# A dense layer's last chunk of 96 units made with 128 columns of weights, and value groups moved to steps 2, 4 and 5

## The chip, the cores and the metric

The kernel runs on one core of a Trainium2 chip. The metric is the device time of one execution in microseconds (us). An execution that is profiled gives a trace: each engine's instructions with their start and duration. The engines are PE (TensorE, matrix products; PEld is its loading of weights), DVE (VectorE), ACT (ScalarE), POOL (GpSimd) and SP (SyncE, which here only issues DMAs).

## What is computed

An input of 2048 tokens with 512 features goes through two layers of recurrent-memory attention, each followed by a dense layer. Cut to what matters:

```
def attention(x, mem):                      # 32 heads of 128; M = 8 memory rows
    for s in range(64):                     # segments of 32 tokens
        h = concat(mem, x[32*s : 32*s+32])  # 40 rows
        q, k, v = h @ Wq, h @ Wk, h @ Wv    # 512 -> 4096 each
        o = (softmax(mask(q @ k.T) * 128**-0.5) @ v) @ Wo
        mem = o[:8]                         # goes on to the next segment
        out[32*s : 32*s+32] = o[8:]
def dense(x):                               # w1: 512 x 1376, w2: 1376 x 512
    return relu(x @ w1) @ w2
x = x + attention(norm(x), mem0);  x = x + dense(norm(x))
x = x + attention(norm(x), mem0);  x = x + dense(norm(x))
```

Both layers use the same weights. A segment needs the memory that the segment before it left, so the segments of one layer are made one after the other.

## The kernel before, in words

**Steps.** The program is unrolled into steps 0 to 67. At step k layer 0 makes segment k (to k = 63) and layer 1 makes segment k - 4 (from k = 4), so steps 4 to 63 carry both layers; steps 0 to 3 and 64 to 67 carry one ("single"). Step 0 is `first_step`, the others are calls of `step(k)` (L895). The order of instructions on PE, DVE, SP and POOL is the one in which the code issues them; the order on ACT is left to a scheduler. Each engine works its list in order, so an instruction that waits holds up all that stand behind it on its engine.

**The recurrent chain.** In each step the 32 heads are made in two halves of 16: queries and keys (`qk`, L575; cast to SBUF by ACT, L581, and DVE, L583), scores (`scores`, L609; added onto a mask that DVE copies into PSUM beforehand, L601), softmax (maximum, subtraction and sum on DVE, exponential on ACT L631, multiplication on POOL or DVE L646), the turning of P (first half by a DMA, second half by PE, L656, with copies L660), then the weighted sum of the values (L682), copied to SBUF (L700), and the output projection of the memory rows (`output_mem`, L617). `new_memory` (L812) copies it (wm, L814), turns it by PE (mt, L820), and copies it into HT and HTm, the inputs of the next step's queries and of the memory's values (`memory_values`, L765).

**Fill.** While the softmax of a half runs, PE does work that does not hang on this chain:
- `output_x(k - 1)`: the output projection of the tokens of the step before (L365, L388 or L393). In steps with k % 4 = 1 there is none, because those tokens went along with the memory rows.
- `dense_h(k - 2)` (L507) and `dense_y(k - 2)` (L528): the two products of the dense layer. The 1376 units are cut into 11 chunks, ten of 128 and the last of 96. `dense_h` makes each chunk with four matmuls (one for each 128 of the 512 features), in pieces of chunks 8 to 10 and 0 to 7; each piece lies in one PSUM bank and is taken to SBUF by ACT with a relu, the chunk of 96 by a relu of its own (L515).
- `values0(p, n)` (L306): the values of layer 0's tokens for a pair of segments p (64 tokens) and 1024 of the 4096 columns: a **value group**, eight matmuls of 64 x 512, copied by ACT (L312) and stored by SP in DRAM (vd0[p]), from where `load_values` reads them when the segment's turn comes. Only odd p are needed. Four groups (n = 0, 2, 4, 6) make one p.

**Which step makes which groups** is written out in `values_at` (L800): step 1 has three, step 5 two, then each step with k % 4 = 1 has three (steps 9 to 37) or four (41 to 61). Steps with two or three groups are `split` ("light"): the dense layer's first piece, half of a group, the second scores, the second piece and the remaining groups follow one another. In steps with four, all of `dense_h` comes before the second scores and the groups after them.

**The inputs.** A tile of 128 tokens, xbs[n], is loaded (SP), its moments are made (`moments_x`, DVE, with a pow on POOL), it is normalized (DVE) and turned into xT0[n], by PE for the first tiles and by a DMA for the others. Before, tile n + 3 of step 4n is loaded at step 4n, its moments are made in step 4n + 1 behind the softmax of the second half, it is normalized at the end of step 4n + 2 and turned in step 4n + 3; tile 3 is turned early, in step 1, into another buffer, and once more in step 3.

Of the kernel before, what the change touches and what calls it, by code (L numbers as in the profile page):

```python
# [22 lines left out]
def kernel(  # L23
# [132 lines left out]
    def load_dense():  # L156
        nc.sync.dma_start(out=w1_sb[:], in_=B_w1.rearrange("(c p) f -> p c f", p=128))
        nc.sync.dma_start(out=w2_sb[:, 0:NFC - 1, :],
                          in_=B_w2[0:(NFC - 1) * 128, :].rearrange("(c p) d -> p c d", p=128))
        nc.sync.dma_start(out=w2_sb[0:F_LAST, NFC - 1, :], in_=B_w2[(NFC - 1) * 128:Dff, :])  # L160

    mhalf_t = const.tile([128, 1], F32)
    nc.vector.memset(mhalf_t[:], -0.5)
# [51 lines left out]
    xT0, xnT_tiles, hT_tiles, vd0, vd1, vmds, wm_tiles, wo_tiles, xp_tiles, vp_tiles, obs = {}, {}, {}, {}, {}, {}, {}, {}, {}, {}, {}  # L215

    def stat_tail(stats, of=""):
        mv = wk.tile([128, 2], F32, tag="ln_mv" + of, bufs=2 - len(of), name="mv")
        nc.vector.bn_aggr(out=mv[:], in_=stats[:])
        rstd = wk.tile([128, 1], F32, tag="ln_rstd" + of, bufs=2 - len(of), name="rstd")  # L220
        nc.vector.tensor_scalar_add(out=rstd[:], in0=mv[:, 1:2], scalar1=LN_EPS)
        nc.gpsimd.tensor_tensor(out=rstd[:], in0=rstd[:], in1=mhalf_t[:], op=ALU.pow)
        return mv, rstd

    def normalize(eng, dst, src, mom, lo, hi):
# [12 lines left out]
            nc.tensor.transpose(tp[:, c4, :], xn[:, c4 * 128:(c4 + 1) * 128], ident[:])  # L238
        return tp

    def inputs_T(n, early=False):
        tag, bufs = ("ob", 1) if early else ("xT0", 3)
        xT0[n] = wk.tile([128, NC4, 128], BF, tag=tag, bufs=bufs, name="xT0")
        if n < 3 or early:
            tp = transpose_pe(xbs[n])
            nc.scalar.copy(out=xT0[n][:], in_=tp[:])
        else:
            nc.sync.dma_start_transpose(out=xT0[n][:], in_=xbs[n][:])
# [47 lines left out]
    def values0(p, n, lo=0, hi=NC4, pool=None, stage=None):  # L296
        r = 64 * (p % 2)
        if (n, lo) == (0, 0):
            vd0[p] = dram.tile([4, 2, 64, 512], BF, tag="vd0", bufs=3, name="vd0")
        if lo == 0:  # L300
            pool, tag = (pool, "wo") if pool else (ps_fill, "fill")
            vp_tiles[p, n] = pool.tile([128, 512], F32, tag=tag, name="vp")
        vp = vp_tiles[p, n]
        for c4 in range(lo, hi):
            for j in range(2):
                nc.tensor.matmul(vp[64 * j:64 * j + 64, :], lhsT=xT0[p // 2][:, c4, r:r + 64],  # L306
                                 rhs=Wv_sb[:, c4, (n + j) * 512:(n + j + 1) * 512],
                                 start=(c4 == 0), stop=(c4 == NC4 - 1), tile_position=(0, 64 * j))
        if hi < NC4:
            return  # L310
        vst = wk.tile([128, 512], BF, tag="vst", bufs=5, name="vst")[:] if stage is None else stage
        nc.scalar.copy(out=vst, in_=vp[:])  # L312
        nc.sync.dma_start(out=vd0[p][n // 2].rearrange("j t e -> (j t) e"), in_=vst)
# [95 lines left out]
    def last_rows(k, eng):  # L409


        r = 64 * (LAST - k)
        R = residual(LAST - 1)
        if not last_t:
            last_t["stats"] = wk.tile([128, 2, 6], F32, tag="ln_last", bufs=1, name="stats")
            last_t["mv"] = wk.tile([128, 2], F32, tag="ln_mvl", bufs=1, name="mv")
            last_t["rstd"] = wk.tile([128, 1], F32, tag="ln_rstdl", bufs=1, name="rstd")
        stats, mv, rstd = (last_t[x][r:r + 64] for x in ("stats", "mv", "rstd"))
        nc.vector.bn_stats(out=stats[:, 0, :], in_=R[r:r + 64, 0:256])
        for j in range(2):  # L420
            nc.vector.tensor_copy(out=last_t["stats"][r + 32 * j:r + 32 * j + 32, 1, :],
                                  in_=last_t["stats"][r + 32 - 32 * j:r + 64 - 32 * j, 0, :])
        nc.vector.bn_aggr(out=mv, in_=stats.rearrange("p n s -> p (n s)"))
        nc.vector.tensor_scalar_add(out=rstd, in0=mv[:, 1:2], scalar1=LN_EPS)
        nc.gpsimd.tensor_tensor(out=rstd, in0=rstd, in1=mhalf_t[r:r + 64, :], op=ALU.pow)
        eng.tensor_scalar(out=XN[r:r + 64, 0:256], in0=R[r:r + 64, 0:256], scalar1=mv[:, 0:1], scalar2=rstd[:, 0:1],
                          op0=ALU.subtract, op1=ALU.mult)
# [58 lines left out]

    def dense_h(d, parts=slice(None)):
        if not 0 <= d <= LAST:  # L490
            return
        lo, hi = span(d)
        n = hi - lo

        def cols(c4):
            return xnT_tiles[d + 2][:, c4, lo:hi]

        if not parts.start:
            hT_tiles[d] = wk.tile([128, NFC, 64], BF, tag="hT", bufs=1, name="hT")
        hT = hT_tiles[d]  # L500
        pieces = ((8, NFC), (0, 4), (4, 8)) if d == LAST - 1 else ((8, NFC), (0, 8))
        for f0, f1 in pieces[parts]:
            hp = ps_fill.tile([128, 8, 64], F32, tag="fill", name="hp")
            for fc in range(f0, f1):
                fs = 128 if fc < NFC - 1 else F_LAST
                for c4 in range(NC4):
                    nc.tensor.matmul(hp[0:fs, fc - f0, 0:n], lhsT=w1_sb[:, c4, fc * 128:fc * 128 + fs],  # L507
                                     rhs=cols(c4), start=(c4 == 0), stop=(c4 == NC4 - 1))
            nfull = min(f1, NFC - 1) - f0
            if (f0, f1) == (4, 8):  # L510
                nc.vector.tensor_scalar_max(out=hT[:, f0:f1, 0:n], in0=hp[:, 0:nfull, 0:n], scalar1=0.0)
            else:
                nc.scalar.activation(out=hT[:, f0:f0 + nfull, 0:n], in_=hp[:, 0:nfull, 0:n], func=ACTF.Relu)
            if f1 == NFC:
                nc.scalar.activation(out=hT[0:F_LAST, NFC - 1, 0:n], in_=hp[0:F_LAST, nfull, 0:n], func=ACTF.Relu)  # L515

    def dense_y(d, f0, f1, bank=1):
        if not 0 <= d <= LAST:
# [261 lines left out]
    def block(k, lo, hi):  # L780
        output_x(k - 1, lo, hi)
        groups = values_at(k)
        if split(k):

            rest = [(i, 0, NC4) for i in range(1, len(groups))]
            if k == 1:
                todo = [] if lo == 0 else [(0, 0, 2)] if hi == 16 else [(0, 2, NC4)] + rest
            else:
                todo = [(0, 0, 2)] if lo == 0 else [(0, 2, NC4)] if hi == 16 else rest
        else:  # L790
            todo = [(i, c4, c4 + 2) for i in range(len(groups)) for c4 in range(0, NC4, 2)
                    if lo < 8 * i + 2 * c4 + 2 <= hi]
        for i, c_lo, c_hi in todo:
            p, n = groups[i]
            values0(p, n, c_lo, c_hi, ps_wo if i in (0, 3 if len(groups) == 4 else 2) else None)

    def split(k):
        return len(values_at(k)) in (2, 3)
# [1 line left out]
    def values_at(k):  # L800


        if k in (1, 5):
            return [(5, 6), (7, 0), (7, 2)] if k == 1 else [(7, 4), (7, 6)]
        if k % 4 != 1 or not has0(k + 1):
            return []
        groups = [(p, n) for p in range(9, NSEG // 2, 2) for n in range(0, NCH, 2)]
        i = k // 4 - 2
        lo = 3 * min(i, 8) + 4 * max(i - 8, 0)
        return groups[lo:lo + (3 if i < 8 else 4)]  # L810

    def new_memory(k, cont, wo):  # L812
        wm_sb = wm_tiles[k] = wk.tile([128, Dm], BF, tag="vst", bufs=5, name="wm")
        nc.scalar.copy(out=wm_sb[:], in_=wo[:])  # L814
        values1(k + 1, 0)
        c = 1 - k % 2
        mt = ps_c.tile([128, NC4, 2, M], F32, tag="c", name="mt")
        for c4 in range(NC4):
# [76 lines left out]
    def step(k):  # L895
        act = layers(k)
        single = len(act) == 1
        cont = [a for a in act if k - DELTA * a + 1 < NSEG]
        n_x = k // 4 + 3
        has_x = n_x < NXT  # L900
        by_pe = k in (1, LAST)
        ahead = has1(k + 1) or not cont
        if k % 4 == 0 and has_x:
            load_xb(n_x)
        with tc.high_priority(offset=PRIO):
            behind = norm_rows.pop(k, None)
            if k == 1:
                def behind():
                    normalize(nc.vector, xbs[n_x], xbs[n_x], moments_x(n_x), 0, 128)
            qks = qk(0, act, behind=behind)  # L910
            load_values(k, act)
            if k == 1:
                memory_values(k)
                inputs_T(n_x, True)
        part = 4 if k == LAST else 8 if single else 5
        mid = 8 if k == LAST else 16

# [46 lines left out]
            add_output(k - 1)  # L964
        if k == LAST:
            add_last(k - 1, 0)
        if k % 4 == 1 and k > 1 and has_x:
            mom["x"] = moments_x(n_x)
        with tc.high_priority(offset=PRIO):
            transpose_p(1)  # L970
# [38 lines left out]
                memory_values(k + 1)  # L1009
        with tc.high_priority(offset=PRIO):  # L1010
            prepare(k + 1)
        if k % 4 == 2 and k > 2 and has_x:
            normalize(nc.vector, xbs[n_x], xbs[n_x], mom["x"], 0, 128)

    mom = {}
    with tc.manual_schedule(engines={mybir.EngineType.PE, mybir.EngineType.DVE, mybir.EngineType.SP,
                                   mybir.EngineType.Pool}):
        load_rest()
        mem0T = const.tile([128, NC4, M], BF)
        tp = transpose_pe(mem0)  # L1020
        nc.vector.tensor_copy(out=mem0T[:], in_=tp[:, :, 0:M])
        for a in range(2):
            nc.vector.tensor_copy(out=HT[:, :, a, 0:M], in_=mem0T[:])
            nc.vector.tensor_copy(out=HTm[:, :, a * M:(a + 1) * M], in_=mem0T[:])
        for n in range(2):
            m = moments_x(n)
            normalize(nc.vector, xbs[n], xbs[n], m, 0, 128)
# [74 lines left out]
```

## Time and profile before

| | us |
|---|---|
| median of 3 runs | 1598.08 |
| lowest and highest | 1596.80 and 1599.88 |
| the profiled execution | 1596.61 |
| its span, first to last instruction | 1594.8 |
| TensorE clock granted | 1.00 of full speed, throughout |

On the page, part 1 has for each engine its busy time, its share of the span and its number of instructions. The groups of instructions read: line, engine, operation, output <- inputs, size of the loaded weights (rows*columns), shape and type, count | busy us, mean ns of one | idle us of the engine just before them, and what ended it. The timeline reads: start (us), time until the end of the last one, engine, line, operation, count, and in brackets the idle time before it. Matmuls overlap and their ends are modelled, so the pace is read from starts. The windows view has a stretch, its length, and for each engine the busy time and the number of instructions, then the granted clock, the DMA share and GB/s.

### The profile page before, as it was taken

Reading aid. Unit: us, or ns where it says so; the run is one execution under the profiler, and the core shown is the slowest. Engines: PE = TensorE matmul, PEld = TensorE weight load, DVE = VectorE, ACT = ScalarE, POOL = GpSimd, SP = SyncE. Lnnn points to the kernel's source line nnn. Section 1 sums busy time; section 2 is a strip of 40 time slices with the busy share of each in tenths; the row PEclk is TensorE's granted clock in tenths of the full one; section 3 lists DMA queues with packets and bytes.
Section 4 is the critical chain, followed back from the end, with each engine's and each line's share of the span. In section 5 each row is a group of like instructions: output and inputs, shape, how many; then the busy total and the mean of one; then the engine's idle time right before and its main releaser. Section 6 shows DMA issues by size and latency. Waiting matters only on the chain.

```text
span 1594.8 us, 94682 instructions
## 1 busy us (share of the span) xinstructions
PE 1565.9 (98%) x42680; PEld 1320.7 (83%) x42680; DVE 1268.4 (80%) x3115; ACT 738.9 (46%) x1799; POOL 349.8 (22%) x670
## 2 busy tenths in 40 slices
PE   6999999999999999999999999999999999999998
PEld 4677888888898888889888888988888898898886
DVE  4578888888888888888888888888878888887866
ACT  3434444444544544454454545445454544545433
POOL 2012222222222222222222222222222222222110
PEclk9999999999999999999999999999999999999999
DMA  9733343343343534444334443343443333233332
GB/s 369 237 78 74 76 87 89 65 98 86 77 78 83 94 64 95 84 73 87 83 87 71 98 83 77 84 83 82 80 98 79 74 88 79 78 77 93 70 75 41
DMA packets 222564, 146.38 MB, mean 92 GB/s; under 512 B 124008, under 2 KB 216528, under 8 KB 222160
## 3 DMA queue, kind: packets, MB, share of 16 engines
q1 hardware_dynamic: 218992, 136.09, 37.6%
q8 instruction: 335, 5.49, 1.5%
q0 software_dynamic: 3072, 4.20, 1.1%
q14 instruction: 69, 0.57, 0.1%
q10 hardware_dynamic: 96, 0.03, 0.0%
HBM read 65.41 MB, written 45.35 MB: 69 GB/s over the span
## 4 chain that ended last, share of the span: by engine, by line
PE 96%; DMA 2%; DVE 1%; SPq 1%; issue 0%; ACT 0%; POOL 0%; POOLq 0%; ACTq 0%
PE qp L575 38%; PE wox L365 10%; PE wo L617 8%; PE vm L765 7%; PE v L346 7%; PE hp L507 6%; PE sp L528 5%; PE pv L682 4%; PE sp L609 4%; PE vp L306 3%; DMA Wv_sb<-in_A_Wv_dram 2%; PE tp L656 1%; PE xp L478 1%; PE wox L388 1%; SPq L134 0%; PE mt L820 0%
## 5 line engine op out<-in xcount | busy, mean ns | idle before, releaser
L581 ACT CAST QT<-qp 128x480 bf16<-128x480 f32 (+3 forms) x408 | 201.7, 494 | 392.3 <-PE qp L575 392.2
L575 PE MATMUL qp<-HT,Wq_sb 128*128 128x80 bf16 (+1 forms) x8704 | 370.2, 200 | 2.1 <-POOL HT L754 1.2
L575 PE MATMUL qp<-HT,Wk_sb 128*128 128x80 bf16 (+1 forms) x8704 | 369.2, 199 | 1.5 <-DMA Wk_sb<-in_A_Wk_dram 0.7
L575 PEld LDWEIGHTS <-Wq_sb 128*128 128x128 bf16 x8704 | 325.6, 100 | 33.8 <-issue 26.5
L575 PEld LDWEIGHTS <-Wk_sb 128*128 128x128 bf16 x8704 | 328.2, 100 | 2.3 <-DMA Wk_sb<-in_A_Wk_dram 1.2
L583 DVE CAST KT<-qp 128x480 bf16<-128x480 f32 (+3 forms) x408 | 231.4, 568 | 124.0 <-PE qp L575 118.1
L646 POOL TENSOR_TENSOR P_sb<-es,sm 128x320 bf16<-128x320 f32 x185 | 130.9, 721 | 751.7 <-ACT es L631 502.2
L365 PE MATMUL wox<-Wo_sb,OTx 128*64 128x256 bf16 x2880 | 173.6, 273 | 0.0
L625 DVE TENSOR_REDUCE mx<-sp 128x8 f32<-128x320 f32 x256 | 115.0, 487 | 73.6 <-PE sp L609 72.7
L365 PEld LDWEIGHTS <-OTx 128*64 128x64 bf16 x2880 | 150.2, 110 | 2.9
L631 ACT ACTIVATE es<-es 128x320 f32<-128x320 f32 x256 | 110.7, 469 | 58.2 <-DVE es L629 57.2
L765 PE MATMUL vm<-Wv_sb,HTm 128*32 128x512 bf16 x2176 | 136.4, 380 | 0.6 <-DVE HT L834 0.6
L641 DVE TENSOR_REDUCE sm<-es 128x8 f32<-128x320 f32 x256 | 118.3, 462 | 15.0 <-ACT es L631 4.7
L617 PE MATMUL wo<-Wo_sb,OTm 128*32 128x512 bf16 x2144 | 128.9, 380 | 0.2 <-issue 0.2
L346 PE MATMUL v<-Wv_sb,xnT 128*32 128x512 bf16 x2048 | 129.0, 378 | 0.0
L601 DVE CAST sp<-maskb 128x320 f32<-128x320 bf16 x256 | 118.4, 484 | 0.0
L629 DVE TENSOR_TENSOR es<-sp,mx 128x320 f32<-128x320 f32 x256 | 113.8, 483 | 1.5
L765 PEld LDWEIGHTS <-HTm 128*32 128x32 bf16 x2176 | 90.6, 96 | 27.4 <-issue 12.3
L528 PE MATMUL sp<-w_sb,hT 128*64 128x256 bf16 (+4 forms) x1452 | 104.1, 275 | 0.2 <-issue 0.2
L769 ACT CAST VmS<-vm 128x512 bf16<-128x512 f32 x134 | 78.6, 587 | 53.8 <-PE vm L765 53.8
L507 PE MATMUL hp<-xnT,w_sb 128*128 128x64 bf16 (+3 forms) x2948 | 102.2, 193 | 0.5 <-DVE xnT L436 0.4
L507 PEld LDWEIGHTS <-w_sb 128*128 128x128 bf16 (+1 forms) x2948 | 95.1, 101 | 1.3 <-issue 0.7
(124 smaller groups left out, 2028.8 us busy)
## 6 DMA issues: line engine op xcount, KB each, us to landing
Vs<-vd SPq DMA_DIRECT2D x96, 256.0 KB
vd<-vst SPq DMA_DIRECT2D x181, 128.0 KB
vmd<-VmS SPq DMA_DIRECT2D x134, 128.0 KB
Vs<-vmd SPq DMA_DIRECT2D x254, 32.0 KB
Vs<-vmd SPq DMA_DIRECT2D x60, 128.0 KB
Wq_sb<-in_A_Wq_dram SPq DMA_DIRECT2D x2, 2048.0 KB
Wk_sb<-in_A_Wk_dram SPq DMA_DIRECT2D x2, 2048.0 KB
Wv_sb<-in_A_Wv_dram SPq DMA_DIRECT2D x2, 2048.0 KB
```

The source lines that it names most:

```text
L346: nc.tensor.matmul(vp[32 * j:32 * j + 32, :], lhsT=tokens[:, c4, :], rhs=Wv_sb[:, c4, n * 512:(n + 1) * 512], start=(c4 == 0), stop=(c4 == ...
L365: nc.tensor.matmul(out[64 * j:64 * j + nr, 0:256], lhsT=lhsT, rhs=rhs[:, 256 * j:256 * j + 256], start=start, stop=stop, tile_position=(0, ...
L507: nc.tensor.matmul(hp[0:fs, fc - f0, 0:n], lhsT=w1_sb[:, c4, fc * 128:fc * 128 + fs], rhs=cols(c4), start=(c4 == 0), stop=(c4 == NC4 - 1))
L528: nc.tensor.matmul(sp_banks[bank][64 * j:64 * j + n, 0:w], lhsT=hT_tiles[d][0:fs, fc, 0:n], rhs=w2_flat[0:fs, fc * Dm + 256 * j:fc * Dm + ...
L575: nc.tensor.matmul(qp[:, hi, 0:ncol], lhsT=W_sb[:, c4, h * Dh:(h + 1) * Dh], rhs=HT[:, c4, a_lo:a_hi, :], start=(c4 == 0), stop=(c4 == NC4 ...
L581: nc.scalar.copy(out=dst[:, 0:nh, a_lo * L:a_hi * L], in_=qp[:, 0:nh, 0:ncol])
L583: nc.vector.tensor_copy(out=dst[:, 0:nh, a_lo * L:a_hi * L], in_=qp[:, 0:nh, 0:ncol])
L601: nc.vector.tensor_copy(out=sp_tiles[a], in_=maskb2)
L617: nc.tensor.matmul(wo[32 * j:32 * j + 32, :], lhsT=OTm[:, h, n, 2 * M * c:2 * M * c + 4 * M], rhs=Wo_sb[:, h, :], start=(h < 4), stop=(h > ...
L641: nc.vector.tensor_reduce(out=sm[:], in_=es[:], axis=AX.X, op=ALU.add)
L646: eng.tensor_tensor(out=P, in0=es[:], in1=sm[:].unsqueeze(2).to_broadcast([128, 8, L]), op=ALU.mult)
L765: nc.tensor.matmul(vp[32 * j:32 * j + 32, :], lhsT=HTm[:, c4, :], rhs=Wv_sb[:, c4, n * 512:(n + 1) * 512], start=(c4 == 0), stop=(c4 == NC ...
```

## The change

- The dense layer's units are numbered anew: the chunk with index 10 becomes units 0 to 95, and chunk c < 10 units 96 + 128c to 223 + 128c. Chunk 10's weights can then be loaded as columns 0 to 127; its 32 surplus results are units that chunk 0 makes as well, and are not read by `dense_y`. The rows of w2 are loaded in the same order. The relu of a piece covers all of its chunks; that of the 96 alone is gone.
- xT0 and the DRAM buffers vd0 have four buffers instead of three. Tile 3 is turned once, by PE in step 1. Every later tile is one round earlier: tile 4 is loaded, gets its moments and is normalized in step 2 and is turned in step 3; tile n + 4 is loaded at step 4n.
- Value groups: step 1 three as before, step 2 one (in `new_memory`, between the copy of wm and its turning), step 4 one (behind the output projection), step 5 three; then three a step to step 49 and four in steps 53, 57 and 61.
- To make room: the moments of a tile share one small tile, the moments of the last segments lie in an `es` buffer, and the initial memory goes from PSUM straight to HT and HTm.

```
     def load_dense():
         nc.sync.dma_start(out=w1_sb[:], in_=B_w1.rearrange("(c p) f -> p c f", p=128))
         nc.sync.dma_start(out=w2_sb[:, 0:NFC - 1, :],
-                          in_=B_w2[0:(NFC - 1) * 128, :].rearrange("(c p) d -> p c d", p=128))
-        nc.sync.dma_start(out=w2_sb[0:F_LAST, NFC - 1, :], in_=B_w2[(NFC - 1) * 128:Dff, :])
+                          in_=B_w2[F_LAST:Dff, :].rearrange("(c p) d -> p c d", p=128))
+        nc.sync.dma_start(out=w2_sb[0:F_LAST, NFC - 1, :], in_=B_w2[0:F_LAST, :])
...
     def stat_tail(stats, of=""):
-        mv = wk.tile([128, 2], F32, tag="ln_mv" + of, bufs=2 - len(of), name="mv")
...
-        rstd = wk.tile([128, 1], F32, tag="ln_rstd" + of, bufs=2 - len(of), name="rstd")
...
+        mom = wk.tile([128, 3], F32, tag="ln_mv" + of, bufs=2 - len(of), name="mv")
+        mv, rstd = mom[:, 0:2], mom[:, 2:3]
...
-    def inputs_T(n, early=False):
-        tag, bufs = ("ob", 1) if early else ("xT0", 3)
-        xT0[n] = wk.tile([128, NC4, 128], BF, tag=tag, bufs=bufs, name="xT0")
-        if n < 3 or early:
+    def inputs_T(n):
+        xT0[n] = wk.tile([128, NC4, 128], BF, tag="xT0", bufs=4, name="xT0")
+        if n < 4:
...
-            vd0[p] = dram.tile([4, 2, 64, 512], BF, tag="vd0", bufs=3, name="vd0")
+            vd0[p] = dram.tile([4, 2, 64, 512], BF, tag="vd0", bufs=4, name="vd0")
...
             for fc in range(f0, f1):
-                fs = 128 if fc < NFC - 1 else F_LAST
+                u = F_LAST + 128 * fc if fc < NFC - 1 else 0
                 for c4 in range(NC4):
-                    nc.tensor.matmul(hp[0:fs, fc - f0, 0:n], lhsT=w1_sb[:, c4, fc * 128:fc * 128 + fs],
+                    nc.tensor.matmul(hp[:, fc - f0, 0:n], lhsT=w1_sb[:, c4, u:u + 128],
                                      rhs=cols(c4), start=(c4 == 0), stop=(c4 == NC4 - 1))
...
-                nc.scalar.activation(out=hT[:, f0:f0 + nfull, 0:n], in_=hp[:, 0:nfull, 0:n], func=ACTF.Relu)
-            if f1 == NFC:
-                nc.scalar.activation(out=hT[0:F_LAST, NFC - 1, 0:n], in_=hp[0:F_LAST, nfull, 0:n], func=ACTF.Relu)
+                nc.scalar.activation(out=hT[:, f0:f1, 0:n], in_=hp[:, 0:f1 - f0, 0:n], func=ACTF.Relu)
...
+        elif k < 5:
+            todo = [(0, 0, NC4)] if k == 4 and lo else []
...
-        if k in (1, 5):
-            return [(5, 6), (7, 0), (7, 2)] if k == 1 else [(7, 4), (7, 6)]
+        if k < 5:
+            return {1: [(5, 6), (7, 0), (7, 2)], 2: [(7, 4)], 4: [(7, 6)]}.get(k, [])
...
-        i = k // 4 - 2
-        lo = 3 * min(i, 8) + 4 * max(i - 8, 0)
-        return groups[lo:lo + (3 if i < 8 else 4)]
+        i = k // 4 - 1
+        lo = 3 * min(i, 12) + 4 * max(i - 12, 0)
+        return groups[lo:lo + (3 if i < 12 else 4)]
...
         values1(k + 1, 0)
+        if k == 2:
+            values0(*values_at(k)[0])
...
-        n_x = k // 4 + 3
+        n_x = k // 4 + 4
...
-        if k % 4 == 0 and has_x:
+        if (k % 4 == 0 or k == 2) and has_x:
             load_xb(n_x)
...
-        if k % 4 == 1 and k > 1 and has_x:
+        if (k % 4 == 1 and k > 1 or k == 2) and has_x:
             mom["x"] = moments_x(n_x)
...
-        if k % 4 == 2 and k > 2 and has_x:
+        if k % 4 == 2 and has_x:
             normalize(nc.vector, xbs[n_x], xbs[n_x], mom["x"], 0, 128)
```

More of the change, by code (lines that the diff above doesn't have):

```diff
@@ L217, in stat_tail @@
     def stat_tail(stats, of=""):
-        mv = wk.tile([128, 2], F32, tag="ln_mv" + of, bufs=2 - len(of), name="mv")
-        nc.vector.bn_aggr(out=mv[:], in_=stats[:])
-        rstd = wk.tile([128, 1], F32, tag="ln_rstd" + of, bufs=2 - len(of), name="rstd")
-        nc.vector.tensor_scalar_add(out=rstd[:], in0=mv[:, 1:2], scalar1=LN_EPS)
-        nc.gpsimd.tensor_tensor(out=rstd[:], in0=rstd[:], in1=mhalf_t[:], op=ALU.pow)
+        mom = wk.tile([128, 3], F32, tag="ln_mv" + of, bufs=2 - len(of), name="mv")
+        mv, rstd = mom[:, 0:2], mom[:, 2:3]
+        nc.vector.bn_aggr(out=mv, in_=stats[:])
+        nc.vector.tensor_scalar_add(out=rstd, in0=mv[:, 1:2], scalar1=LN_EPS)
+        nc.gpsimd.tensor_tensor(out=rstd, in0=rstd, in1=mhalf_t[:], op=ALU.pow)
         return mv, rstd
@@ L414, in last_rows @@
         if not last_t:
-            last_t["stats"] = wk.tile([128, 2, 6], F32, tag="ln_last", bufs=1, name="stats")
-            last_t["mv"] = wk.tile([128, 2], F32, tag="ln_mvl", bufs=1, name="mv")
-            last_t["rstd"] = wk.tile([128, 1], F32, tag="ln_rstdl", bufs=1, name="rstd")
+            t = wk.tile([128, 8 * L], F32, tag="es", bufs=2, name="lm")
+            last_t["stats"] = t[:, 0:12].rearrange("p (n s) -> p n s", n=2)
+            last_t["mv"] = t[:, 12:14]
+            last_t["rstd"] = t[:, 14:15]
         stats, mv, rstd = (last_t[x][r:r + 64] for x in ("stats", "mv", "rstd"))
@@ L504, in dense_h @@
             for fc in range(f0, f1):
-                fs = 128 if fc < NFC - 1 else F_LAST
+                u = F_LAST + 128 * fc if fc < NFC - 1 else 0
                 for c4 in range(NC4):
-                    nc.tensor.matmul(hp[0:fs, fc - f0, 0:n], lhsT=w1_sb[:, c4, fc * 128:fc * 128 + fs],
+                    nc.tensor.matmul(hp[:, fc - f0, 0:n], lhsT=w1_sb[:, c4, u:u + 128],
                                      rhs=cols(c4), start=(c4 == 0), stop=(c4 == NC4 - 1))
-            nfull = min(f1, NFC - 1) - f0
             if (f0, f1) == (4, 8):
-                nc.vector.tensor_scalar_max(out=hT[:, f0:f1, 0:n], in0=hp[:, 0:nfull, 0:n], scalar1=0.0)
+                nc.vector.tensor_scalar_max(out=hT[:, f0:f1, 0:n], in0=hp[:, 0:f1 - f0, 0:n], scalar1=0.0)
             else:
-                nc.scalar.activation(out=hT[:, f0:f0 + nfull, 0:n], in_=hp[:, 0:nfull, 0:n], func=ACTF.Relu)
-            if f1 == NFC:
-                nc.scalar.activation(out=hT[0:F_LAST, NFC - 1, 0:n], in_=hp[0:F_LAST, nfull, 0:n], func=ACTF.Relu)
+                nc.scalar.activation(out=hT[:, f0:f1, 0:n], in_=hp[:, 0:f1 - f0, 0:n], func=ACTF.Relu)
     def dense_y(d, f0, f1, bank=1):
@@ L794, in block @@
             p, n = groups[i]
-            values0(p, n, c_lo, c_hi, ps_wo if i in (0, 3 if len(groups) == 4 else 2) else None)
+            values0(p, n, c_lo, c_hi, ps_wo if k % 4 == 1 and i in (0, 3 if len(groups) == 4 else 2) else None)
     def split(k):
@@ L908, in behind @@
                 def behind():
-                    normalize(nc.vector, xbs[n_x], xbs[n_x], moments_x(n_x), 0, 128)
+                    normalize(nc.vector, xbs[3], xbs[3], moments_x(3), 0, 128)
             qks = qk(0, act, behind=behind)
@@ L913, in step @@
                 memory_values(k)
-                inputs_T(n_x, True)
+                inputs_T(3)
         part = 4 if k == LAST else 8 if single else 5
@@ L1018 @@
         load_rest()
-        mem0T = const.tile([128, NC4, M], BF)
         tp = transpose_pe(mem0)
-        nc.vector.tensor_copy(out=mem0T[:], in_=tp[:, :, 0:M])
         for a in range(2):
-            nc.vector.tensor_copy(out=HT[:, :, a, 0:M], in_=mem0T[:])
-            nc.vector.tensor_copy(out=HTm[:, :, a * M:(a + 1) * M], in_=mem0T[:])
+            nc.vector.tensor_copy(out=HT[:, :, a, 0:M], in_=tp[:, :, 0:M])
+            nc.vector.tensor_copy(out=HTm[:, :, a * M:(a + 1) * M], in_=tp[:, :, 0:M])
         for n in range(2):
```

## The prediction

> **What bounds the kernel now.** I read the page's first part and its chain of waits, to see which engine sets the end:
>
> ```profile
> PE 1565.9 (98%) x42680; PEld 1320.7 (83%) x42680; DVE 1268.4 (80%) x3115; ACT 738.9 (46%) x1799; POOL 349.8 (22%) x670
> PE 96%; DMA 2%; DVE 1%; SPq 1%; issue 0%; ACT 0%; POOL 0%; POOLq 0%; ACTq 0%
> ```
>
> TensorE is busy for 98% of the span and is 96% of the chain that ended last. So an edit pays only where it shortens TensorE's own stream, or fills a place where TensorE stood still. Next, the groups of instructions with shapes kept apart, for the dense layer's first product (L507):
>
> ```profile
> L507 PE MATMUL hp<-xnT,w_sb 128*128 128x64 bf16 x2440 | 91.5, 193 | 0.5 <-DVE xnT L436 0.4
> L507 PEld LDWEIGHTS <-w_sb 128*128 128x128 bf16 x2680 | 87.8, 98 | 1.3 <-issue 0.7
> L507 PE MATMUL hp<-xnT,w_sb 128*96 128x64 bf16 x244 | 21.0, 209 | 0.0
> L507 PEld LDWEIGHTS <-w_sb 128*96 128x96 bf16 x268 | 17.3, 125 | 0.0
> ```
>
> The narrower load is the slower one: 125 ns for 96 columns against 98 for 128. The busy column exaggerates it: 21.0/244 = 86 ns against 91.5/2440 = 37 ns seems to promise 244 x 49 ns = 12 us, but a group of four ends in a 0.2 us pipeline tail that the next matmuls overlap. What counts is the distance from start to start, which the timeline of TensorE gives, first in step 29 (dense layer cut in two), then in step 41 (in one piece):
>
> ```profile
> 703.81 0.58 PE L507 MATMUL hp<-xnT,w_sb 128*128 128x64 bf16 x12
> 704.32 0.62 PE L306 MATMUL vp<-Wv_sb,xT 128*64 128x512 bf16 x4
> ...
> 705.27 1.11 PE L507 MATMUL hp<-xnT,w_sb 128*128 128x64 bf16 x32
> 706.31 1.92 PE L306 MATMUL vp<-Wv_sb,xT 128*64 128x512 bf16 x16
> 708.06 1.18 PE L528 MATMUL sp<-w_sb,hT 128*64 128x320 bf16 x18
> ```
> ```profile
> 982.98 1.51 PE L507 MATMUL hp<-xnT,w_sb 128*128 128x64 bf16 x44
> 984.42 0.57 PE L609 MATMUL sp<-KT,QT 128*40 128x40 bf16 x32
> ```
>
> 44 matmuls take 1.44 us, 12 take 0.51, and the 32 more are all wide: 0.93/32 = 29 ns each. 32 wide ones with the hand-over to the next line take 1.04, so the hand-over is 0.11. The 12 are 8 wide and 4 narrow: (0.51 - 8 x 0.029 - 0.11)/4 = 42 ns. Single starts in the trace read 45 and 29 ns, and these I use.
>
> Last, the windows view by whole steps (length, then busy TensorE), for steps 33, 41, 5 and 4:
>
> ```profile
> 786.57:809.53 22.96, 22.95 (x605) 18.54 (x604) 19.15 (x47) 12.16 (x29) 5.66 (x11) 1.00 0.38 97
> 972.69:996.13 23.44, 23.44 (x612) 18.55 (x612) 19.14 (x47) 12.79 (x30) 5.66 (x11) 1.00 0.47 97
> 133.76:156.66 22.90, 22.07 (x596) 17.79 (x596) 19.14 (x47) 11.31 (x28) 5.05 (x10) 1.00 0.46 87
> 110.14:133.76 23.62, 22.54 (x711) 18.92 (x708) 20.19 (x52) 10.46 (x27) 4.74 (x9) 1.00 0.36 82
> ```
>
> Three value groups: 22.96; four: 23.44; two: 22.90, with TensorE idle for 0.83. Where there are two, the softmax and not TensorE sets the length. Step 4 has none and is idle for 1.08.
>
> **The change, part by part.**
>
> *The padded chunk.* Four loads a step go from 96 to 128 columns: 4 x (45 - 29) = 64 ns off TensorE. This is a gain only where TensorE itself is late. In steps 4 to 63 the narrow loads stand before the second half's scores, whose last keys were cast 0.2 us (light steps, such as 29) to 0.7 us before them, and what follows the scores does not shrink: 60 x 0.064 = 3.8. In steps 2, 3, 65 and 66 dense_h stands between the scores and the transposes of P, where the softmax ends last or level: nothing. Step 64 has fill to spare: 0.06. At the end, the third dense piece waits for the buffer that two relus (278 + 211 ns) free; one relu of 128x192 takes about 0.33 (the 128x192 copy by ScalarE, 331 ns): some 0.1 less. Sum **-4.0**; bounds -4.4 and, if waits take its place, 0. The 67 relus saved cost TensorE nothing now: ScalarE is busy for 46%.
>
> A rule that speaks against this: the Trainium skill, TensorE: Matmul & The Clock Gate, section LDWEIGHTS (loading the stationary operand), says that a load's time scales with its columns, P/1.2 ns; an estimate by that page is 80 ns for 96 columns and 107 for 128, and a sum on the slower side (the third rival below). The same page, section Weight-path perf modes — Fast Weight Load (FWL) and DoubleRow, says that a fast path is on when the number of weights is exactly 128; by that the pad gains, as in the sum here. The rows above, 125 and 98 ns, agree with the second.
>
> *Steps 41, 45 and 49 from four groups to three.* The group is eight matmuls, 1.75/16 x 8 = 0.88 us, but the three-group step stands still for part of that, and the windows give the net: 23.44 - 22.96 = 0.48 each (step 45 was 23.62). Sum **-1.5**; bounds -1.3 and -1.7. Steps 53, 57 and 61 keep four; steps 9 to 37 keep three.
>
> *Step 5 from two to three:* 22.90 to 22.96, the eight matmuls lying in the 0.83 of idle: **+0.1**.
>
> *Step 4, one group* ahead of the second dense product:
>
> ```profile
> 124.06 1.21 PE L528 MATMUL sp<-w_sb,hT 128*32 128x320 bf16 x18
> 126.21 0.48 PE L656 MATMUL tp<-ident,P_sb 128*64 128x80 bf16 x16 [0.94 <-POOL HT L754]
> ```
>
> TensorE idles 0.94 before the transposes, and starts of L528 would move by 0.88: **0**. Its copy on ScalarE (0.59) stands between the exponentials, over at 124.5, and the copy of P at 126.6. If that cover were gone it would cost 0.9.
>
> *Step 2, one group and the moments of input tile 4.* Both are new there. VectorE gets statistics, aggregate and add (0.69 + 0.18 + 0.15, some 1.05 with gaps) between the multiplication of P and the copy of the turned P:
>
> ```profile
> 83.81 0.49 DVE L646 TENSOR_TENSOR P_sb<-es,sm 128x320 bf16<-128x320 f32 x1
> 85.10 0.49 DVE L660 CAST PT_sb<-tp 128x320 bf16<-128x320 f32 x1 [0.81 <-PE tp L656]
> ```
>
> 84.30 + 1.05 = 85.4, so the copy is 0.3 late, and weighted values, output and memory behind it. The group stands where TensorE waits for wm:
>
> ```profile
> 87.67 0.39 PE L528 MATMUL sp<-w_sb,hT 128*32 128x256 bf16 x4
> 88.53 0.27 PE L820 MATMUL mt<-sel,wm 128*32 128x16 bf16 x16 [0.47 <-ACT wm L814]
> ```
>
> Some 0.65 lies between the last start of L528 and L820, against 0.88: +0.2. *Step 3* begins with the normalization of that tile (0.40, L227) on VectorE, queued ahead of the first cast of keys; in step 3 that cast is late already (key matmuls of the second batch stand still 0.15 behind it), so +0.4. Together **+0.9**; bounds 0 (all hidden) and 0.88 + 1.05 + 0.40 = 2.3. The tile's load goes on SP's queue behind the VmS stores (issued to 73.4) and ahead of Vs <- vd, which lands in time for L682 at 85.0; so it is there by 84.3, and each load behind it is issued some 0.5 later, with 7 us to spare. The pow on POOL (0.56) has until step 3.
>
> *At nothing:* four copies from PSUM in place of one and four small ones (0.17 each, in a prologue that waits for Wv's second half at 37.7); one tile for both moments (same instructions); the fourth xT0 and vd0 buffer (they remove waits and one of 13 transposing DMAs); the last moments in an es buffer that nothing writes any more; w2's rows in another order, in DMAs of equal size. In steps 48 to 51 VectorE loses the work that step 2 gains, but there nothing waits for it.
>
> **Sum:** -4.0 - 1.5 + 0.1 + 0 + 0.9 = -4.5. The profiled execution took 1596.61 (span 1594.8 and 1.8 around it): 1592.1. It lies 1.5 under the median of the runs, 1598.08 (1596.80 to 1599.88), so against the median I forecast **1593.6**. A difference of 0.2%, 3.2 us, is about what a measurement of this kernel can tell from no change.
>
> **Rivals.**
>
> *Waits take the chunk's place.* Scores would have to wait 64 ns longer for keys or masks. For: in light steps the second mask ends at 704.90, about 0.1 before its scores. Against: 0.7 of slack in most others. All of it: 0 - 1.5 + 0.1 + 0.9 = -0.5, 1597.6.
>
> *The early steps cost nothing:* wm's wait and idle VectorE hide everything: -5.4, 1592.7; with the lower ends of the first two terms as well -6.0, 1592.1. For: the windows view has VectorE busy for 11.66 of step 2's 19.92 us. Against: the in-order queue at 84.3.
>
> *Loads priced by columns (slower).* If the padded load kept to the slow path, its pace would go from 45 to 45 x 128/96 = 60 ns: 244 x 15 = +3.7, the sum +3.2, **1601.3**. It decides from a pace of 47 ns, where the sum is 0. Against: the same line's 2680 loads of 128 columns, from the same tile, at 98 ns. This is the rule of the section on LDWEIGHTS named above, put into the trace's pace.
>
> *The busy column is right:* 12 us off the chunk, 1585.6. Against: the start-to-start count above.
>
> **How the numbers follow.** Forecast 0.65 (its own range 1592 to 1595.8; 0.55 of it under 1594.9, 0.10 above); waits 0.14; early steps free 0.12; loads by columns 0.04; busy column 0.01; an unseen wait in the early steps of 2 us or more 0.04, half of it slower. Faster by over 0.2%: 0.55 + 0.12 + 0.01 = 0.68; slower 0.04 + 0.02 = 0.06; within 0.2%: 0.26. The range, 1590.6 to 1597.0, takes in -6.0 with the runs' spread of 1.3 below, and above most of the way to the waits.
>
> **What would show it.** Right: all 2948 loads of L507 at 98 ns; the runs of 44 at 1.37; steps 4n, 4n+2, 4n+3 about 0.06 shorter; steps 41, 45, 49 at 22.9; step 4 at 23.6; steps 2 and 3 longer by 0.9 together. Wrong: scores (L609) waiting for KT or the mask; L507's loads at 125 or more; step 2 with a wait of VectorE for xb.

## The result, and the profile after

| | before | after |
|---|---|---|
| median of 6 runs each, us | 1597.88 | 1592.76 |
| lowest and highest | 1596.80 to 1601.47 | 1591.91 to 1593.72 |
| ratio, with its 95% interval | | 0.9964 (0.9953 to 0.9975) |
| the profiled execution, and its span | 1596.61, 1594.8 | 1592.97, 1591.3 |

The change makes the kernel 5.1 us faster (ratio 0.9964; 4.0 to 7.5 us by the interval). The forecast was 4.5.

The page's first part and its chain, in the kernel after: TensorE is still 96% of the chain, its busy time is 3.1 us less, and ScalarE has 67 instructions fewer (the relus of the chunk of 96).

```profile
PE 1562.8 (98%) x42680; PEld 1317.4 (83%) x42680; DVE 1268.5 (80%) x3114; ACT 734.5 (46%) x1732; POOL 349.8 (22%) x670
PE 96%; DMA 2%; DVE 1%; SPq 1%; issue 0%; ACT 0%; POOL 0%; POOLq 0%
```

The groups of the dense layer's first product (now L508). There is one kind of load, 128 columns at 98 ns; the rows of 96 columns are gone:

```profile
L508 PEld LDWEIGHTS <-w_sb 128*128 128x128 bf16 x2948 | 90.9, 98 | 1.9 <-issue 1.1
L508 PE MATMUL hp<-xnT,w_sb 128*128 128x64 bf16 x2684 | 90.5, 193 | 0.4 <-DVE xnT L436 0.4
```

TensorE's timeline, the 44 matmuls of `dense_h` in step 10 and what follows them: 261.75 - 260.38 = 1.37 us, where before it was 1.44.

```profile
260.38 1.45 PE L508 MATMUL hp<-xnT,w_sb 128*128 128x64 bf16 x44
261.75 0.57 PE L607 MATMUL sp<-KT,QT 128*40 128x40 bf16 x32
```

The same in step 29, a light one. The twelve matmuls take 0.44 us from start to start instead of 0.51. The scores (L607) take 0.55 us to the next line, where before they took 0.49: they now wait for the second mask, as the first rival said. But `dense_y` (L526) waits less before the transposes (L654), 1.13 us from its first start against 1.19 before, because the softmax that it waits for had begun earlier too. So the 0.06 that the mask takes back is given again, and the step is 0.06 shorter. First the two lines of before that these distances are taken from, beside those that the prediction shows, then the kernel after:

```profile
704.78 0.56 PE L609 MATMUL sp<-KT,QT 128*40 128x40 bf16 x32
...
709.25 0.48 PE L656 MATMUL tp<-ident,P_sb 128*64 128x80 bf16 x16
```
```profile
701.92 0.52 PE L508 MATMUL hp<-xnT,w_sb 128*128 128x64 bf16 x12
702.36 0.62 PE L305 MATMUL vp<-Wv_sb,xT 128*64 128x512 bf16 x4
702.82 0.62 PE L607 MATMUL sp<-KT,QT 128*40 128x40 bf16 x32
703.37 1.11 PE L508 MATMUL hp<-xnT,w_sb 128*128 128x64 bf16 x32
...
706.16 1.18 PE L526 MATMUL sp<-w_sb,hT 128*64 128x320 bf16 x18
707.29 0.48 PE L654 MATMUL tp<-ident,P_sb 128*64 128x80 bf16 x16
```

The windows view by whole steps, for steps 33, 41, 5 and 4. Steps 33 and 41 have become alike, three groups each; step 5 has three in the length of two, with TensorE no longer idle (22.90 of 22.90 busy, before 22.07); step 4 has one more group and is not longer (before 23.62).

```profile
785.27:808.16 22.89, 22.89 (x607) 18.53 (x604) 19.14 (x47) 12.12 (x28) 5.65 (x11) 1.00 0.41 95
971.24:994.16 22.92, 22.92 (x604) 18.52 (x604) 19.17 (x47) 12.12 (x28) 5.65 (x11) 1.00 0.45 94
134.29:157.19 22.90, 22.90 (x604) 18.23 (x604) 19.13 (x47) 11.83 (x28) 5.04 (x10) 1.00 0.44 92
110.77:134.29 23.52, 23.43 (x719) 19.12 (x715) 20.24 (x52) 10.98 (x27) 4.74 (x9) 1.00 0.39 88
```

Where the time went, from the steps of the two traces:

| | forecast | measured |
|---|---|---|
| steps 6 to 63, the padded chunk (medians of alike steps: 0.065, 0.070, 0.072, 0.069 shorter for k % 4 = 0 to 3) | -3.7 | -4.0 |
| padded chunk elsewhere: steps 3 and 4 about 0.08 each, 64, 65 and 66 about 0.06 each, the last piece of step 67 0.12 | -0.3 | -0.5 |
| steps 41, 45, 49 from four groups to three, without the chunk's part: 0.46, 0.66, 0.46 | -1.5 | -1.6 |
| steps 4 and 5, the groups | +0.1 | 0 |
| step 2: the group, and the moments | +0.5 | +0.44 + 0.03 |
| step 3: the late cast of keys | +0.4 | +0.3 |
| sum | -4.5 | -5.3 |

The spans differ by only 3.5. The rest is in short stops of TensorE, a few tenths of a microsecond to one each, that the profile puts down to "issue". In steps 6 to 63 they are at other places in each execution (1.6 us together before, 2.7 after), and the medians of the steps do not contain them. In step 2 every one of the twelve profiles has some, 0.6 us or more. So the rows of steps 2 and 3 are read between instructions and not from the lengths: step 2 as a whole took 19.92 us before and 19.72 after. One stop, 0.6 us in the middle of `dense_h` in step 3 of the kernel after, is in no row of the table:

```profile
100.35 0.58 PE L508 MATMUL hp<-xnT,w_sb 128*128 128x32 bf16 x17
101.36 0.21 PE L508 MATMUL hp<-xnT,w_sb 128*128 128x32 bf16 x2 [0.44 <-issue]
```

A stop of 0.3 to 0.6 us stands in that line in five of the seven profiled kernels that make a group in step 2, and in none of the five that make none. Whether it is a further price of that group, no run settles. An experiment of one run is read below by its steps, not by its span.

### The profile page after: what moved, and what is told of

The parts are those of the page before. It is cut to its first block, busy times and chain, and to the rows that moved or that the text cites. A ratio compares the mean times of both kernels' runs of the same rounds, so it can differ in the third digit from the quotient of the medians.

```text
span 1591.3 us, 94609 instructions
## 1 busy us (share of the span) xinstructions
PE 1562.8 (98%) x42680; PEld 1317.4 (83%) x42680; DVE 1268.5 (80%) x3114; ACT 734.5 (46%) x1732; POOL 349.8 (22%) x670
## 4 chain that ended last, share of the span: by engine, by line
PE 96%; DMA 2%; DVE 1%; SPq 1%; issue 0%; ACT 0%; POOL 0%; POOLq 0%
PE qp L573 38%; PE wox L364 10%; PE wo L615 8%; PE vm L763 7%; PE v L345 7%; PE hp L508 5%; PE sp L526 5%; PE pv L680 4%; PE sp L607 4%; PE vp L305 3%; DMA Wv_sb<-in_A_Wv_dram 2%; PE tp L654 1%; PE xp L478 1%; PE wox L387 1%; SPq L134 0%; PE mt L822 0%
## 5 line engine op out<-in xcount | busy, mean ns | idle before, releaser
L526 PE MATMUL sp<-w_sb,hT 128*64 128x256 bf16 (+4 forms) x1452 | 104.1, 276 | 0.2 <-issue 0.2
L508 PE MATMUL hp<-xnT,w_sb 128*128 128x64 bf16 (+1 forms) x2948 | 98.5, 192 | 0.8 <-issue 0.4
L513 ACT ACTIVATE hT<-hp 128x192 bf16<-128x192 f32 (+3 forms) x134 | 60.0, 448 | 70.8 <-PE hp L508 70.6
```

Source lines behind the costliest of these rows:

```text
L508: nc.tensor.matmul(hp[:, fc - f0, 0:n], lhsT=w1_sb[:, c4, u:u + 128], rhs=cols(c4), start=(c4 == 0), stop=(c4 == NC4 - 1))
L526: nc.tensor.matmul(sp_banks[bank][64 * j:64 * j + n, 0:w], lhsT=hT_tiles[d][0:fs, fc, 0:n], rhs=w2_flat[0:fs, fc * Dm + 256 * j:fc * Dm + ...
```

## The experiments

Theory: the chunk of 96 columns costs 16 ns a load more on TensorE than one of 128, that is the whole gain of the chunk, and the groups' move gains 1.5 in late steps and gives 0.9 back in steps 2 and 3. Rivals: waits, the relus, or a price by columns.

### The two parts, each alone

The padded chunk alone: the kernel before, with w2's rows, the loads and the relu of the kernel after, and nothing else of the change.

> The kernel before with the padded chunk alone (and the one relu that goes with it). Theory, the load's pace counts and nothing else: 64 ns less in each of steps 4 to 63, steps with three and four groups alike, so about 4.0 to 4.3 us less than before, 1593.7. Rival, waits take the place of the load: step lengths unchanged, within 0.5 us of before. Rival, busy column: 12 us less. Rival, loads priced by columns: 3.7 us more.

The groups and the tiles alone: the kernel after, with these parts put back.

```
+                fs = 128 if fc < NFC - 1 else F_LAST
...
+                    nc.tensor.matmul(hp[0:fs, fc - f0, 0:n], lhsT=w1_sb[:, c4, fc * 128:fc * 128 + fs],
```

> The kernel after with the chunk of 96 back as it was (96 columns, a relu of its own), so that the value groups and the earlier input tiles are alone. Theory: steps 41, 45 and 49 shorter by 0.48 to 0.55 each, steps 2 and 3 longer by 0.8 together, the others as before: 0.5 to 0.8 us less than before, not to be told from it in the times. Rival, the groups carry the gain: 3 us or more less.

The chunk alone: 1593.40 us (median of 5) against 1598.99 of the kernel before (15 runs), ratio 0.9968 (0.9955 to 0.9980), 3.2 to 7.2 us. Its steps 6 to 63 are 0.059 to 0.066 shorter than before by their medians, 3.7 us in all, as forecast; of the 4.0 in the first row of the table 0.3 is therefore not the chunk's alone. The groups alone: 1598.47 (11 runs), ratio 1.0002 (0.9993 to 1.0011). So what can be measured of the gain is the chunk's. In the trace of the groups alone, steps 41, 45 and 49 are 0.46, 0.62 and 0.47 shorter than before, the group in step 2 costs 0.44 and the late cast in step 3 0.31, as in the kernel after: a net gain of 0.7, which lies inside that interval. This is a gain of steps read one by one, not a measured gain of time.

### Are the relus a part of it?

The chunk padded, but with the relu of the 96 units kept apart:

```
+                    nc.tensor.matmul(hp[:, fc - f0, 0:n], lhsT=w1_sb[:, c4, u:u + 128],
...
             if f1 == NFC:
                 nc.scalar.activation(out=hT[0:F_LAST, NFC - 1, 0:n], in_=hp[0:F_LAST, nfull, 0:n], func=ACTF.Relu)
```

> The kernel before with the padded chunk, but the relu still cut in two (128 rows for the full chunks, 96 for the last). It tells the load from the relu. Theory: steps 4n, 4n+2 and 4n+3 as with one relu, 23.34, 23.32 and 23.24; only the last dense piece at the end, which waits for a buffer, is some 0.1 us later. Rival, the saved relu on ScalarE is what shortens the steps: 23.41, 23.39 and 23.30 as before.

One run, 1594.07. Its steps' medians for k % 4 = 0 to 3 (23.345, 22.893, 23.322, 23.235) are those of the padded chunk alone (23.348, 22.895, 23.325, 23.236) to 3 ns. In the steps the saved relus are worth nothing. At the end of step 67 the cut relu costs 0.05 us: the last `dense_h` takes 1.60 us to the next line, against 1.55 with one relu.

### The price of a load, by its width

A second chunk with 96 columns, in the kernel before:

```
-                fs = 128 if fc < NFC - 1 else F_LAST
+                fs = 128 if fc < NFC - 2 else F_LAST
...
```

> The kernel before with one chunk more made narrow: of chunk 9 only 96 of its 128 units are made, the 32 others are left out of the sum. The suspected cost is doubled. Theory: the four loads of chunk 9 go from 29 to 45 ns from start to start, each step of 4 to 63 is 64 ns longer than before (4n: 23.47, 4n+3: 23.36), some 4 us in all. Rival, waits: step lengths as before. Rival, columns priced: 64 ns shorter or the same.

1603.01 in one run. By their medians its steps are 0.065, 0.061, 0.059 and 0.060 longer than before: the same price a second time, also where the first rival had put waits. Another 1.75 of it is step 4, where the clock fell (last section).

The kernel after with another width of the last chunk's loads:

```
-                u = F_LAST + 128 * fc if fc < NFC - 1 else 0
+                u, fs = (F_LAST + 128 * fc, 128) if fc < NFC - 1 else (0, 112)
...
```

> The kernel after, but the last chunk is loaded with 112 columns; 16 of them are surplus and not read, nothing is left out. Priced by columns on the slow side: 45 x 112/96 = 52 ns from start to start, 92 ns a step over after (4n+3: 23.33). One price for all that isn't 128 wide: 45 ns (23.30). If 128 isn't special and the rate merely falls with width: under 45 ns.

> The kernel after, but the last chunk is loaded with 64 columns; 32 of its 96 units are left out. It measures how the slow load's price goes with the width. If a load under 128 columns is priced by its columns: 45 x 64/96 = 30 ns from start to start, the step as after (4n+3: 23.24). If every load that isn't 128 wide pays one price: 45 ns, the step as before (23.30).

One run of each. 112 columns: 1600.81, the steps 6 to 63 are 0.093 to 0.094 longer than after by their medians; a further 1.6 is step 2, where the clock fell (last section). 64 columns: 1612.89, steps 0.35, 0.05, 0.27 and 0.35 longer for k % 4 = 0 to 3. That 64 columns are the dearest was in no theory. The rows of the load in the groups, first with 112 columns, then with 64:

```profile
L508 PEld LDWEIGHTS <-w_sb 128*112 128x112 bf16 x268 | 19.1, 132 | 0.0
```
```profile
L508 PEld LDWEIGHTS <-w_sb 128*64 128x64 bf16 x268 | 13.4, 110 | 3.3
```

The load of 64 columns is shorter than that of 112 (and, at 110 ns, still longer than the full one), so it is not the load. The 44 matmuls of step 10 take 264.09 - 262.48 = 1.61 us with 64 columns:

```profile
262.48 1.68 PE L508 MATMUL hp<-xnT,w_sb 128*128 128x64 bf16 x44
264.09 0.58 PE L610 MATMUL sp<-KT,QT 128*40 128x40 bf16 x32
```

The single starts tell where: inside the chunk they are 32 ns apart, but from the last wide matmul to the first of 64 columns it is 123 ns, and 128 from the last of 64 to the next wide one, where 29 is the pace. The first is the hand-over of 0.11 us that the prediction read off before the value group (L306), whose weights have 64 columns. Ahead of the scores, whose weights have 40, it stands in the kernel before too (124 ns). In `dense_y`, the product with the 64 rows of this chunk costs a further 0.12. In the light steps (0.05) the chunk stands ahead of a value group, whose weights have 64 columns too, so that the hand-over between them was due anyway. To tell the width from the kind, 80 columns:

```
+                u, fs = (F_LAST + 128 * fc, 128) if fc < NFC - 1 else (0, 80)
...
```

> The kernel after, its last chunk made with 80 columns of weights (units 80 to 95 are left out, and the relu of the last chunk stands alone). With 64 columns the distance of starts within the chunk was 32 ns, but entering and leaving the chunk cost 94 and 99 ns, like the hand-over to the 40-column scores; with 112 columns it was 52 ns and there was no hand-over. Theory (the load sets the pace at about 0.47 ns a column, and the hand-over belongs to a switch to matmuls of 64 columns or fewer): starts 37 to 38 ns apart, no hand-over, the run of 44 at 1.41 us against 1.38 after, steps 0.03 longer than after, span near 1593. Rival (every narrowing brings a hand-over, the wider it is the later it shows): entering or leaving costs 50 ns or more, the run of 44 over 1.5 us. Second rival (anything over 64 columns takes a fixed slow path): starts 45 ns apart or more, the run of 44 at 1.44 or more.

```profile
L508 PEld LDWEIGHTS <-w_sb 128*80 128x80 bf16 x268 | 15.5, 121 | 0.0
```

1596.22 in one run, a span of 1594.5 where 1593 was expected; most of the difference is in stops. Steps are 0.036 to 0.040 longer than after by their medians, there is no hand-over, and the first theory holds:

| columns of weights | load, ns | start to start, ns | 44 matmuls, us | hand-over |
|---|---|---|---|---|
| 64 | 110 | 32 | 1.61 | in and out, 94 and 99 ns |
| 80 | 121 | 38 | 1.42 | none |
| 96 | 125 | 45 | 1.44 | none |
| 112 | 132 | 52 | 1.47 | none |
| 128 | 98 | 29 | 1.38 | none |

From 64 to 112 columns the pace follows the columns, 0.46 to 0.50 ns each; by that 128 would be 60. It is 29.

### The price of the early steps

The moments of tile 4 made later in step 2 (behind the copies of the attention output), its normalization still in step 2:

```
+        if k == 2:
+            mom["x"] = moments_x(n_x)
         if single and k < LAST and ahead:
...
             add_output(k - 1, 0)
+            if k == 2:
+                normalize(nc.vector, xbs[n_x], xbs[n_x], mom["x"], 0, 128)
```

> The kernel after; the moments of input tile 4 stand in step 2 behind the copies of the outputs, and its normalization stands there too, not at the head of step 3. Theory: step 3 loses the 0.31 us that its second batch of keys waits for the late cast, step 2 gains at most 0.1. Rival, step 3's extra is a wait for something else (its input transposes, or a stop without a recorded cause): its second batch still stands still for 0.49.

1593.26 in one run. The second batch of keys in step 3 starts on time again (0.32 less), but in step 2 the copies of the turned memory (L833, L836) now stand behind the normalization on VectorE, 0.12 late, and two short stops take the rest. The cast was the cause of step 3's wait; the way out costs a third of it.

The same with one more group early: step 0 makes one, and step 53 three instead of four.

```
+            return {0: [(5, 6)], 1: [(7, 0), (7, 2), (7, 4)], 2: [(7, 6)], 4: [(9, 0)]}.get(k, [])
...
```

> The kernel of the run with the moments and normalization in step 2, and one value group more ahead of step 5: (5, 6) in step 0 while TensorE waits for wm there, (7, 0), (7, 2) and (7, 4) in step 1, (7, 6) in step 2, (9, 0) in step 4, so that only steps 57 and 61 have four. Theory: step 53 0.50 shorter, step 0 at most 0.3 longer since it waits there for 0.9: 0.2 to 0.5 less than without, some 0.6 less than after, 1592.2. Rival, step 0 has no room: it is 0.9 longer and nothing is won.

1594.70 (11 runs), ratio 0.9976 (0.9967 to 0.9985) against the kernel before: not better than the kernel after, whose interval it overlaps. Step 53 is 0.44 shorter, where 0.50 was expected. Step 0 takes 1.66 us from the start of the last output projection to the turning of the memory, 1.32 in the kernel after, so the group there costs 0.34, where at most 0.3 was expected. What is left, 0.1, is less than the runs differ by. In the profiled execution the stops of steps 6 to 63 add 3.9 us, against 2.7 after; whether that holds for the median of the runs, one profile does not show.

The kernel after without the group in step 2, which step 4 makes instead; step 49 has four again:

```
+            return {1: [(5, 6), (7, 0), (7, 2)], 4: [(7, 4)]}.get(k, [])
...
```

> The kernel after without the value group in step 2: step 4 makes that group, step 5 the next one and two more, and step 49 has four groups again; nothing is left out. The early loading, moments and normalization of input tile 4 stay. Theory (the group in step 2 costs 0.44 us between the output projection of the memory and its turning, the late first cast of keys in step 3 belongs to the normalization): in step 2 the stretch from the end of that projection to the turning goes back from 1.30 to 0.86 us; the second key batch of step 3 still stands 0.49 us; step 49 is 0.48 longer; the sum is about nothing, span within 2 us of after (1591.3) by the short stops that differ from run to run. Rival (the group's copy by ScalarE and its store are what make step 3 late): the stall in step 3 goes back to 0.18 as well, a gain of 0.3 more.

1593.86 in one run. TensorE's timeline in steps 2 and 3:

```profile
87.90 0.39 PE L526 MATMUL sp<-w_sb,hT 128*32 128x256 bf16 x4
88.77 0.27 PE L822 MATMUL mt<-sel,wm 128*32 128x16 bf16 x16 [0.47 <-ACT wm L816]
...
94.17 0.56 PE L573 MATMUL qp<-HT,Wq_sb 128*128 128x40 bf16 x16 [0.31 <-DVE KT L581]
```

From the first of these lines to the second it is 0.87 us, as before; with the group it is 1.30 (next section). The wait of 0.31 for the keys stays: it is the normalization's, not the group's. Step 49 is 0.49 longer than after. The stop in `dense_h` of step 3 is not there. So a group in step 2 costs 0.44 (without that stop) and saves 0.49: it is worth nothing that could be measured, while those in steps 4 and 5 are free.

## Why the prediction was right, step by step

**What bounds the kernel, and the 16 ns.** Right. Both the busy column (12 us promised) and the mean of the load would have misled; start to start gave 45 and 29 ns, and every experiment on the width but that with 64 columns, where the hand-overs come on top, moved the steps by four times its difference of starts.

**A gain only where TensorE is late.** Right for steps 6 to 63; wrong for steps 3, 65 and 66, put at nothing. In step 3 `dense_h` is 0.08 shorter (1.275 to 1.195 us with half as many tokens, where a wide matmul takes 25 ns and a narrow one still 45), in 65 and 66 it is 0.06 shorter, and the steps with it: TensorE was late there too, 0.2 us in all. Step 5 went the other way: it was counted with 0.064 and gains nothing (22.90 with the chunk alone, as before), because its softmax ends last.

**Waits take the chunk's place.** The wait that was named is there (0.06 in the scores of the light steps) and takes nothing, for the reason shown with step 29: what waits behind it had waited for the same softmax.

**Loads priced by columns.** Wrong at 128 columns, right below. The Trainium skill, TensorE: Matmul & The Clock Gate, section LDWEIGHTS (loading the stationary operand), has a load's time grow with its columns; from 80 to 112 the trace agrees in kind (121, 125 and 132 ns, starts 38, 45 and 52 ns apart), but 128 columns fall out of it (98 and 29), and there the measurement decides. Section Weight-path perf modes — Fast Weight Load (FWL) and DoubleRow of the same page has a fast path when the number of weights is exactly 128; the break between 112 and 128 agrees with it.

**Groups to three.** Right (1.6 for 1.5). **Step 4, at nothing.** Right. The group fills the idle time, and the transposes (L654) no longer stand still ahead of their start, for which before 0.94 was noted:

```profile
124.83 1.05 PE L305 MATMUL vp<-Wv_sb,xT 128*64 128x512 bf16 x8
125.81 1.19 PE L526 MATMUL sp<-w_sb,hT 128*32 128x320 bf16 x18
126.93 0.48 PE L654 MATMUL tp<-ident,P_sb 128*64 128x80 bf16 x16
```

**Steps 2 and 3, +0.9.** The sum was near (0.78), but two of its terms were not, and that one was too low and the other too high by about the same is luck. The group was put at 0.2 and cost 0.44: it starts 0.32 behind L526 and takes 0.88, but the matmuls that follow it (L822) start another 0.1 later, which looks like the hand-over that the prediction counted for `dense_h` and left out here (the weights change from 64 columns to 32). TensorE in the kernel after:

```profile
87.02 0.39 PE L526 MATMUL sp<-w_sb,hT 128*32 128x256 bf16 x4
87.34 1.05 PE L305 MATMUL vp<-Wv_sb,xT 128*64 128x512 bf16 x8
88.32 0.27 PE L822 MATMUL mt<-sel,wm 128*32 128x16 bf16 x16
```

The moments were put at 0.3 and cost 0.03. VectorE in the kernel after:

```profile
83.04 0.49 DVE L644 TENSOR_TENSOR P_sb<-es,sm 128x320 bf16<-128x320 f32 x1
83.45 0.69 DVE L232 BATCH_NORM_STATS2 stats<-xb 128x6 f32<-128x512 bf16 x1
...
84.46 0.48 DVE L658 CAST PT_sb<-tp 128x320 bf16<-128x320 f32 x1
```

The prediction let the statistics start at the end of the multiplication, 0.49 after its start; they start 0.41 after it, and the copy 1.01 behind them: 1.42 in all, against 1.29 before. Of the 0.13 that this leaves, the weighted values behind the copy show 0.03 (0.11 in the groups alone). The starts, not the durations, add up on VectorE too. Step 3's 0.4 was 0.3, the wait of 0.31 seen above.

**The early steps cost nothing.** This rival named 1592.7, nearer to the measured median of 1592.76 than the forecast of 1593.6. It is wrong all the same: the 0.44 and the 0.31 stand in the trace. The runs of one kernel differ by 2 us and more, so the median cannot choose between the two.

## What to carry to other kernels

Price a matmul that is short in its moving columns by the distance of starts, not by its busy time, and look at what its weights cost: here weights of 128 columns went faster than 80, 96 or 112, so rounding a chunk up was a gain of 16 ns for each matmul. A block of work that is to fill a wait must be counted with the hand-over to the next kind of matmul; in a wait of 0.65 us a block of 0.88 cost 0.44, and in one of 0.94 it was free. When moved work gains half a microsecond here and gives it back there, read both at the instructions concerned: a median of runs whose spread is 2 us tells neither, and the length of a step with stops of its own does not either.

## What the runs showed of the hardware that was not expected

- A change from weights of 128 columns to 64 or 40 costs 94 ns, and one from 64 back to 128 costs 99, on top of the pace of 29; changes between 128 and 80, 96 or 112 columns have no such cost.
- In step 4 of two of the four profiled kernels that make no group there, TensorE was granted about half its clock for some 3.4 us behind its idle time, and the step was 1.7 longer. The windows view of the padded chunk alone (the third figure from the end is the clock):

```profile
126.00:128.00 2.00, 1.85 (x88) 1.48 (x92) 1.93 (x8) 1.17 (x6) 0.43 (x3) 1.00 0.03 8
128.00:130.00 2.00, 2.00 (x26) 0.85 (x28) 1.96 (x8) 0.86 (x4) 0.00 (x0) 0.54 0.00 0
130.00:132.00 2.00, 2.00 (x28) 0.81 (x24) 0.32 (x1) 0.54 (x1) 0.60 (x1) 0.61 0.00 0
```

  It begins some 2 us after the idle time ended. None of the eight with a group in step 4 shows it there; one (112 columns) shows it in step 2, as long after a stop of 1.1 us, but two others with a stop of 1.0 and 1.1 us at that place do not. Whether the group in step 4 keeps the clock up, and so makes the runs of the kernel after lie closer together, twelve profiles do not settle.
- The short stops put down to "issue" add 1.3 to 3.9 us to steps 6 to 63 of an execution, at other places each time. What sets them stays open.
